# Starting the global queries' steps and the second unit of four heads four slots later in each chunk

## The chip, the cores and the metric

The kernel runs on one core of one Trainium2 chip. The metric is the device time of one execution in microseconds (us). A core has a tensor engine for matmuls (TensorE, PE in the profile), VectorE (DVE), ScalarE (ACT), GpSimd (POOL) and a sync engine (SP), which here issues nearly all DMAs. Each engine works through its own list of instructions in order, and waits for others by semaphores.

## The reference

Attention of 8 batches with 8 heads of 64, with 512 local and 32 global tokens each, and then a gated feed-forward layer over all 4608 tokens.

```python
k_all = concatenate([k_g, k_l]); v_all = concatenate([v_g, v_l])
out_g = matmul(sm(scale * matmul(q_g, k_all.T)), v_all)      # global queries see all keys
s_ll = where(abs(i - j) <= 32, scale * matmul(q_l, k_l.T), -1e9)
s_lg = scale * matmul(q_l, k_g.T)
out_l = matmul(sm(concatenate([s_lg, s_ll])), v_all)          # local queries: a band and the global keys
x = rows of concatenate([out_g, out_l])                       # 4608 x 512
xn = x / sqrt(mean(x * x) + 1e-6) * rms_g
g = xn @ w_gate                                               # 512 x 1536
out = (g / (1 + exp(-g)) * (xn @ w_val)) @ w_out
```

Here `sm` is a softmax with the row's maximum subtracted. `-1e9` stands for the mask outside the band.

## The kernel before

The 4608 rows go through the feed-forward layer in nine chunks: chunks 0 to 7 are the 512 local rows of each batch, chunk 8 the 256 global rows of all batches. While the matmuls of chunk c run, the attention for chunk c+1 is woven in between them. The order of every engine's instructions is the order in which the program writes them: chunk 0, with the attention of batches 0 and 1, by a list of names (`ORDER`), and the rest by the loop at the end of `attention_moe_kernel`, lines 1180 to 1209.

**Slots.** That loop has 72 slots for a chunk of 512 rows. Each slot writes one piece of the feed-forward layer, six matmuls of 128x512. Slots 0 to 47 are the twelve `f` (128 columns of the hidden layer each): two slots for the gate product, then ACT's `tanh` and DVE's `gate` (line 970); two for the value product, then DVE's `inner` (line 977), ACT's rounding to 16 bits (line 980) and POOL's rest (line 151). The products are on line 959. Slots 48 to 71 are four output blocks of six slots (line 1014), with a store after slots 53, 59, 65 and 71. After a slot's matmuls the attention steps that are due are written (`slot()`), and then the slot's own ACT and DVE work.

**Units and steps.** The attention of chunk c+1 is up to three units: local heads 0 to 3, the global queries of one batch, local heads 4 to 7. `UNIT` says from which slot a unit may start; after that each step follows its predecessors at fixed distances.

- A local unit: L and V (loads of q, k, v), S (scores, line 648, four slots after L), for each of four score banks M and N (masked minimum on DVE at line 599, exponentials on ACT at line 610), D (division, POOL, line 625) and T (transpose on DVE, line 630); A and B (the products with v in two parts, line 691, into four banks `a`); X and Y (DVE copies two of these banks each into a tile `x`, line 704, ACT squares it, line 708, and POOL adds up the squares, line 710).
- A global unit: GL (loads), GS (scores, line 762, into four banks `gs`), GM and GN (softmax, line 774 and 784), GT (transposes, line 805), GA (products with v, line 819), GD (division), GX (transpose into `xg`).

By these distances the steps of the three units stood so in each of chunks 1 to 6: first local unit L 2, S 6, A 19, B 21, X 22, Y 24; global unit GL 19, GS 23, GM 24, GN 26, GT 29, GA 33, GD 34, GX 36; second local unit L and V 33, S 37, T 43 to 49, A 50, B 52, X 53, Y 55. At the end of slot 55 what is left of the units is written at once. In chunk 7 two global units run alone, from slots 0 and 20 (`UNIT[2]`).

**Banks.** Scores, transposes and attention outputs share four PSUM banks (the pool tag `pa`). The global scores need all four, and so do a local unit's scores and its outputs.

**Norm.** The norm of chunk c+1 is written at slot 59 (DVE: transpose of the sum of squares and a reduce, lines 922 and 924), 61 (PE: sum over partitions, line 933, then DVE's root steps from line 934 on) and 66 (scaling, and splitting into two 16-bit halves `xh` and `xl`).

Of the kernel before, what the change touches and what calls it, by code (L numbers as in the profile page):

```python
# [65 lines left out]
def attention_moe_kernel(  # L66
# [24 lines left out]
    SPLIT, BGAP = 5, 2  # L91
    GG = (4, 5, 4, 3)
    NORM = (56, 59, 61, 66)
    UNIT = {2: (0, 20), 3: (2, 19, 33)}
    ST = 6
    con = ctx.enter_context(tc.tile_pool(name="con", bufs=1))
    pool = ctx.enter_context(tc.tile_pool(name="pool", bufs=2))
# [1012 lines left out]
    for c in range(NCH):  # L1110
# [3 lines left out]
        for i, un in enumerate(units):  # L1114
# [6 lines left out]
            for name, fn, pe, after in steps:  # L1121
                st = {"name": name, "fn": fn, "pe": pe, "c": c, "x": xi, "after": [], "at": None}
                st["from"] = UNIT[len(units)][i]
                for dep, gap in after:
# [211 lines left out]
```

## Time and profile before

| | |
|---|---|
| median of 3 runs | 981.94 us (979.61 to 983.16) |
| the profiled execution | 978.9 us, of which its span 977.1 us |
| granted TensorE clock, mean | 0.99 |
| TensorE products, line 959, xh and xl groups | 503.2 + 318.0 us |
| TensorE output blocks, line 1014 | 237.4 us |
| DMA | 88.24 MB, 90 GB/s over the span |

Busy times of matmuls overlap one another, because they are pipelined and their ends are modelled; distances between starts are the safer measure. A row of a timeline gives the start in us from the start of the span, the duration, the engine, the line, the operation, its output and inputs, the count, and in brackets the idle time ahead of it with what ended it. A row of the list of waits gives who waited for whom: us in total, times, the longest.

### The profile page before, as it was taken

How to read it: one execution, taken by the hardware profiler on the slowest of the kernel's cores; microseconds unless marked ns; L12 is line 12 of the kernel's file. 1: busy time of each engine (PE TensorE's matmuls, PEld its weight loads, DVE VectorE, ACT ScalarE, POOL GpSimd, SP SyncE). 2: the span in 40 equal slices, each digit the busy share in tenths (PEclk: the TensorE clock that was granted, in tenths of full speed). 3: DMA queues.
4: the chain of work that ended last, by engine and by line, in shares of the span. 5: the costliest groups of instructions: out<-in, count | busy, mean ns of one | idle time of the engine just before them, and what ended most of it. 6: DMA issues, size and time to landing. Idle time of an engine off the chain costs nothing.

```text
span 977.1 us, 22949 instructions
## 1 busy us (share of the span) xinstructions
PE 939.2 (96%) x9732; PEld 486.3 (50%) x9732; DVE 451.0 (46%) x1369; ACT 409.2 (42%) x1070; POOL 194.4 (20%) x183
## 2 busy tenths in 40 slices
PE   6588999999999999999999999999999999999998
PEld 4444455445544544445444544455444544444584
DVE  6999973444244344434345244434334344232331
ACT  7999982434124341435124441435034431332131
POOL 0000000232213231223113140323114140111120
PEclk9799999999999999999999999999999999999999
DMA  9962421800044000710053001700062002400100
GB/s 355 406 261 93 152 88 38 269 31 2 23 167 116 16 2 33 254 32 1 23 188 110 2 12 44 233 31 2 23 212 85 2 13 82 142 1 1 40 5 22
DMA packets 31254, 88.24 MB, mean 90 GB/s; under 512 B 3632, under 2 KB 3888, under 8 KB 31152
## 3 DMA queue, kind: packets, MB, share of 16 engines
q1 hardware_dynamic: 30720, 86.46, 25.7%
q8 instruction: 76, 1.25, 0.5%
q10 hardware_dynamic: 432, 0.33, 0.1%
q14 instruction: 26, 0.21, 0.1%
HBM read 77.86 MB, written 8.91 MB: 89 GB/s over the span
## 4 chain that ended last, share of the span: by engine, by line
PE 86%; DVE 6%; DMA 5%; ACT 2%; issue 1%; SPq 0%; ACTq 0%; DVEq 0%
PE p L959 48%; PE po L1014 24%; PE a L691 3%; PE po L1081 3%; PE s L648 2%; DMA k<-in_qk_dram 2%; DMA v<-in_vw_dram 1%; DMA wr<-in_w_in_dram 1%; PE ga L819 1%; PE gt L805 1%; PE gs L762 1%; DVE wf L366 1%; ACT wr L265 1%; DMA gkq<-in_gkq_dram 1%; DVE t L1050 1%
## 5 line engine op out<-in xcount | busy, mean ns | idle before, releaser
L959 PE MATMUL p<-xh,wf 128*128 128x512 f16 (+1 forms) x1728 | 503.2, 368 | 8.3 <-DVE t L1050 6.3
L959 PEld LDWEIGHTS <-wf 128*128 128x128 f16 x2592 | 250.5, 98 | 280.1 <-issue 20.4
L959 PE MATMUL p<-xl,wf 128*128 128x512 f16 (+1 forms) x864 | 318.0, 368 | 0.0
L1014 PE MATMUL po<-wo,h 128*128 128x512 f16 x1080 | 237.4, 379 | 0.0
L151 POOL TENSOR_TENSOR h<-t,h 128x512 f16<-128x512 f32 (+1 forms) x96 | 105.2, 1095 | 565.9 <-ACT h L980 528.6
L1014 PEld LDWEIGHTS <-h 128*128 128x128 f16 x1080 | 104.8, 98 | 123.7
L970 DVE SCALAR_TENSOR_TENSOR t<-t,p 128x512 f32<-128x512 f32 (+1 forms) x96 | 62.8, 654 | 223.3 <-ACT t L969 223.3
L980 ACT CAST h<-t 128x512 f16<-128x512 f32 (+1 forms) x96 | 56.5, 588 | 164.8 <-DVE t L977 164.8
L969 ACT ACTIVATE t<-p,half_inv 128x512 f32<-128x512 f32 (+1 forms) x96 | 62.9, 656 | 115.8 <-PE p L959 100.5
L977 DVE SCALAR_TENSOR_TENSOR t<-t,c_h,p 128x512 f32<-128x512 f32 (+1 forms) x96 | 68.1, 710 | 78.6 <-PE p L959 78.6
L610 ACT ACTIVATE e<-e,sm 128x128 f32<-128x128 f32 x192 | 74.8, 390 | 40.6 <-DVE sm L599 40.6
L625 POOL TENSOR_TENSOR e<-e,sm 128x512 f32<-128x512 f32 x48 | 49.9, 1039 | 45.5 <-DVE sm L624 32.8
L1025 ACT ACTIVATE o<-po,kk 128x512 f32<-128x512 f32 x15 | 10.3, 688 | 114.2 <-PE po L1014 114.2
L599 DVE CUSTOM_DVE_ANT_0 e<-s,maskb 128x128 f32<-128x128 f32 x192 | 45.0, 281 | 5.6 <-PE s L648 5.6
L1027 DVE TENSOR_SCALAR o<-po,kk 128x512 f32<-128x512 f32 x15 | 11.3, 751 | 64.5 <-PE po L1014 64.5
L708 ACT ACTIVATE sq<-x 128x512 f32<-128x512 f32 x24 | 15.1, 628 | 55.7 <-DVE x L704 55.5
L630 DVE STREAM_TRANSPOSE et<-e 128x512 f32<-128x512 f32 x48 | 34.0, 708 | 7.5 <-POOL e L625 7.5
L691 PEld LDWEIGHTS a<-et,v 32*64 32x64 f32 x2112 | 31.0, 130 | 11.0 <-issue 10.2
L610 ACT ACTIVATION_READ_ACCUMULATOR e<-e,sm 128x1 f32 x192 | 35.8, 186 | 0.0
L691 PE MATMUL a<-et,v 32*64 32x96 f32 (+3 forms) x2112 | 35.5, 258 | 0.0
L704 DVE COPY x<-a 128x256 f32<-128x256 f32 x48 | 17.5, 416 | 38.2 <-PE a L691 38.2
L1081 PE MATMUL po<-wo,h 128*128 128x512 f16 x144 | 32.4, 379 | 0.0
(320 smaller groups left out, 743.5 us busy)
## 6 DMA issues: line engine op xcount, KB each, us to landing
wr<-in_w_in_dram SPq DMA_DIRECT2D x24, 512.0 KB, 10.0
k<-in_qkb_dram SPq DMA_DIRECT2D x24, 448.0 KB, 7.5
gkq<-in_gkq_dram SPq DMA_DIRECT2D x16, 576.0 KB, 8.0
out_dram<-o SPq DMA_DIRECT2D x34, 256.0 KB, 2.0
v<-in_vb_dram SPq DMA_DIRECT2D x24, 352.0 KB, 5.1
v<-in_vw_dram SPq DMA_DIRECT2D x16, 512.0 KB, 9.6
gv<-in_gv_dram SPq DMA_DIRECT2D x16, 448.0 KB, 10.9
wr<-in_w_out_dram SPq DMA_DIRECT2D x12, 512.0 KB, 4.1
```

The lines of the kernel that those rows point to most:

```text
L151: nc.gpsimd.tensor_tensor(dst, a, b, ALU.subtract)
L599: nc.vector.tensor_tensor_reduce(out=e[:, g, :], in0=ps[:, g * P : (g + 1) * P], in1=late["mask"][:, m * P : (m + 1) * P], scale=-0.125, s ...
L610: nc.scalar.activation(e[:, g, :], e[:, g, :], AF.Exp, bias=sm[:, 0, j + g : j + g + 1], scale=-1.0, accum_out=sm[:, 1, j + g : j + g + 1],)
L625: nc.gpsimd.tensor_tensor(e, e, r.unsqueeze(2).to_broadcast([P, 4, P]), ALU.mult)
L691: nc.tensor.matmul(o, st["v"][x][r, m * D : (m + 1) * D], e, start=(m == blocks[0]), stop=(m == blocks[-1]), skip_group_check=True,)
L959: nc.tensor.matmul(ps[:, :n], wf[f][:, a, o : o + P], ch[z][k][:, :n], start=(k == 0 and i == 0), stop=(k == NK - 1 and i == 2),)
L969: nc.scalar.activation(t[:, :n], pg[:, :n], AF.Tanh, scale=half_inv[:, f : f + 1])
L970: nc.vector.scalar_tensor_tensor(t[:, :n], t[:, :n], 1.0, pg[:, :n], ALU.add, ALU.mult)
L977: nc.vector.scalar_tensor_tensor(t[:, :n], t[:, :n], c_h[:, f : f + 1], pv[:, :n], ALU.mult, ALU.mult)
L980: nc.scalar.copy(h[:, 0, :n], t[:, :n])
L1014: nc.tensor.matmul(ps[0], ch["h", f][:, a, j * P : (j + 1) * P], wo[f][:, z, :], start=(f == 0 and q == 0), stop=(f == NF - 1 and q == 2),)
L1081: nc.tensor.matmul(po[j], ch["h", f][:, a, j * P : (j + 1) * P], wo[f][:, z, :], start=(f == 0 and q == 0), stop=(f == NF - 1 and q == 2),)
```

## The change

One line: in chunks 1 to 6 the global unit may start from slot 23 instead of 19, and the second local unit from slot 37 instead of 33.

```diff
-    UNIT = {2: (0, 20), 3: (2, 19, 33)}
+    UNIT = {2: (0, 20), 3: (2, 23, 37)}
```

By the fixed distances GS stands at slot 27, GX at 40, the second unit's S at 41, T at 47 to 53, A at 54. B would be due at 56, X at 57 and Y at 59; all three are written at the end of slot 55. Work, tiles and buffers stay as they are.

The first place is on DVE in chunk 1, from the copies of the first unit's step X to the first softmax step of the global unit (`a` are the local outputs in PSUM, `gs` the global scores, `p_5` and `p_6` the products of f=5 and f=6). Before:

```order
L704 COPY x_0_2602<-a_2474 128x256
L977 SCALAR_TENSOR_TENSOR t_2592<-t_2592,c_h,p_5_2595 128x512
L704 COPY x_1_2645<-a_2475 128x256
L704 COPY x_1_2645<-a_2476 128x256
L774 ISA ge_2614,gsm_2613<-gs_2615,zeros 128x272
L774 ISA gsm_2613 128x1
L774 ISA ge_2614,gsm_2613<-gs_2616,zeros,gsm_2613 128x272
```

and now:

```order
L704 COPY x_0_2592<-a_2474 128x256
L977 SCALAR_TENSOR_TENSOR t_2582<-t_2582,c_h,p_5_2585 128x512
L704 COPY x_1_2623<-a_2475 128x256
L704 COPY x_1_2623<-a_2476 128x256
L970 SCALAR_TENSOR_TENSOR t_2635<-t_2635,p_6_2616 128x512
L977 SCALAR_TENSOR_TENSOR t_2635<-t_2635,c_h,p_6_2638 128x512
L774 ISA ge_2652,gsm_2651<-gs_2653,zeros 128x272
```

The copies stay behind the `inner` of f=5; the readers of the global scores moved behind the whole of f=6.

On PE the same place, with the semaphores that the rows wait for: the last product of the slot ahead of the global scores, and the first score of each half. Before:

```order
L959 MATMUL p_5_2595<-xh_2172,wf_957 128x512
L762 MATMUL gs_2615<-gkq_2517 32x272 [waits DMAHW3_49,DVE_49]
L762 MATMUL gs_2617<-gkq_2517 32x272 [waits DVE_49]
...
L762 MATMUL gs_2616<-gkq_2517 32x272 [waits DVE_49,PE_49]
L762 MATMUL gs_2618<-gkq_2517 32x272 [waits DVE_49,PE_49]
```

and now:

```order
L959 MATMUL p_6_2638<-xh_2172,wf_1124 128x512
L762 MATMUL gs_2653<-gkq_2603 32x272 [waits DMAHW3_49,PE_49]
L762 MATMUL gs_2655<-gkq_2603 32x272 [waits PE_49]
...
L762 MATMUL gs_2654<-gkq_2603 32x272 [waits DVE_49,PE_49]
L762 MATMUL gs_2656<-gkq_2603 32x272 [waits DVE_49,PE_49]
```

The scores follow the products of f=6 instead of those of f=5, and their first half no longer has a wait for DVE.

The last place is on ACT in chunk 1, from the second unit's last step before its outputs to the norm's split (`po` are output blocks 0 and 2, `x_2` and `x_3` the second unit's outputs). Before:

```order
L980 CAST h_2992<-t_3022 128x512
L708 ACTIVATE sq_3177<-x_2_3174 128x512
L1025 ACTIVATE o_3180<-po_3044,kk 128x512
L708 ACTIVATE sq_3199<-x_3_3196 128x512
L1025 ACTIVATE o_3286<-po_3233,kk 128x512
```

and now:

```order
L619 ACTIVATE sm_2870<-sm_2870 128x4
L1025 ACTIVATE o_3082<-po_3028,kk 128x512
L708 ACTIVATE sq_3193<-x_2_3190 128x512
L708 ACTIVATE sq_3199<-x_3_3196 128x512
L1025 ACTIVATE o_3286<-po_3233,kk 128x512
```

The store of block 0 is written ahead of both squares, which now come together, and the last of the softmax (line 619) comes after the last `f` instead of before it. On SP the order of the DMAs is the same before and now.

## The prediction

> **What bounds the kernel now.** First the page: the share of each engine, then the list of who waited for whom on the tensor engine alone, then one chunk in windows.
>
> ```profile
> PE 939.2 (96%) x9732; PEld 486.3 (50%) x9732; DVE 451.0 (46%) x1369; ACT 409.2 (42%) x1070; POOL 194.4 (20%) x183
> PEclk9799999999999999999999999999999999999999
> PE gs L762 <- DVE x L704: 3.9, 6, 0.7
> PE p L959 <- issue: 1.4, 1, 1.4
> 281.90:390.60 108.70, 108.05 (x1167) 53.51 (x1166) 45.23 (x145) 38.84 (x115) 28.10 (x25) 1.00 0.22 72
> ```
>
> TensorE (PE) is busy 96% of the span at its full granted clock; the digits below 9 stand at the start. From 174 us to the end its list has only the two rows shown (us in total, times, longest). The last row is one of the six chunks that the change touches, from window start to end: length, PE busy, weight loads, DVE, ACT, POOL, granted clock, DMA share and GB/s. PE is idle in it for 0.65 us out of 108.70. So VectorE (DVE), ScalarE (ACT) and GpSimd (POOL), at 45, 39 and 28 us, bound nothing by their work; the change can gain only where PE stalls, six times at the global queries' scores (line 762), and can lose only where it makes PE stall anew.
>
> Here is that stall in the same chunk: PE's timeline, then DVE's, then PE's at the second global unit of the last-but-one chunk, which no local unit runs beside.
>
> ```profile
> 316.98 0.38 PE L959 MATMUL p<-xh,wf 128*128 128x512 f16 x1
> 317.29 0.69 PE L762 MATMUL gs<-gkq 64*32 64x272 f32 x16
> 318.62 1.02 PE L762 MATMUL gs<-gkq 64*32 64x272 f32 x16 [0.65 <-DVE x L704]
> 319.57 0.39 PE L959 MATMUL p<-xh,wf 128*128 128x512 f16 x1
> ...
> 317.39 0.75 DVE L977 SCALAR_TENSOR_TENSOR t<-t,c_h,p 128x512 f32<-128x512 f32 x1 [1.80 <-PE p L959]
> 318.06 0.75 DVE L704 COPY x<-a 128x256 f32<-128x256 f32 x2
> ...
> 861.35 1.15 PE L762 MATMUL gs<-gkq 64*32 64x272 f32 x32
> 862.43 0.39 PE L959 MATMUL p<-xh,wf 128*128 128x512 f16 x1
> ```
>
> The scores come as 32 records. After the first 16 PE stops until DVE has copied the last two local output banks out of PSUM (step Y, issued in slot 24). Those copies stand behind the `inner` multiplication of line 977, which needs the products of slot 23 itself, and the scores were queued right after those products. So PE waits for work that it releases only just before.
>
> **The change part by part.** A slot is six 128x512 matmuls, and I take its price from this unit's end:
>
> ```profile
> 355.32 4.05 PE L1014 MATMUL po<-wo,h 128*128 128x512 f16 x18
> 359.30 1.54 PE L691 MATMUL a<-et,v 32*64 32x256 f32 x80
> 360.77 2.76 PE L1014 MATMUL po<-wo,h 128*128 128x512 f16 x12
> 363.47 1.31 PE L691 MATMUL a<-et,v 32*64 32x96 f32 x96
> 364.71 11.83 PE L1014 MATMUL po<-wo,h 128*128 128x512 f16 x54
> 376.37 0.29 PE L933 MATMUL ss<-nt,same 128*128 128x16 f32 x2
> ```
>
> The 54 matmuls take 376.37 - 364.71 = 11.66 us from start to start: 0.216 us each, 1.30 us a slot.
>
> *Global scores, slot 23 to 27.* No matmul is added or taken away. The copies of step Y stay at slot 24; at 318.06 to 318.81 they will be done 3 slots (3.9 us) before the scores come up. The wait goes. Its price is not the 0.65 us of the wait row but what the group takes from its first matmul to the next product: 319.57 - 317.29 = 2.28 us with the wait, 862.43 - 861.35 = 1.08 us without. In both places the product ahead starts 0.31 us before the group, so the comparison is fair. The stall costs 1.20 us, and in six chunks 7.2 us. What could be late next: the scores' own input, and PE's waits behind them. Line 970 of f=6 and all later products sit 4 slots apart from the global steps as before, since one f takes four slots; a shift by four meets the same phase of the gates. Products of f=6 now carry waits on DVE of their own (the wait of the scores covered them), for `inner` of f=5, which ends at 318.14, two slots before the second product group that needs the bank: hidden.
>
> *Why 1.20 and not 0.65.* [...] This trace speaks for starts: two groups of the same 32 records differ by 1.20.
>
> *Loads.* The steps GL, L and V are moved four slots as well, with five, four and two DMA issues. Their order on the sync engine's (SP's) queue stays as it is, and that queue doesn't run by slots:
>
> ```profile
> 284.96 0.90 SPq L741 DMA_DIRECT2D gkq<-in_gkq_dram  x2
> 285.90 1.84 SPq L747 DMA_DIRECT2D gv<-in_gv_dram  x3
> 293.24 0.43 SPq L580 DMA_DIRECT2D k<-in_qkb_dram  x1
> 314.72 1.61 SPq L588 DMA_DIRECT2D v<-in_vb_dram  x2
> gkq<-in_gkq_dram SPq DMA_DIRECT2D x16, 576.0 KB, 8.0
> gv<-in_gv_dram SPq DMA_DIRECT2D x16, 448.0 KB, 10.9
> ```
>
> The global tiles are requested at 285, 32 us before their scores, and land in 8 to 11 us. The second local unit's last load is issued at 314.72, when the first unit's step B, which doesn't move, frees its tile. Cost nothing; if the queue did follow the slots, the scores would still have their gap of four slots, 5.2 us, against 8.0, and 2.8 us x 6 would be lost. Nothing in SP's queue holds it back, so I don't count that.
>
> *Second local unit, scores slot 37 to 41, A 50 to 54, B 52 to 55, X 53 to 55, Y stays at 55.* Up to A everything moves by four slots, 5.2 us. From slot 48 on PE does output blocks and DVE and ACT have no gates, so the softmax ends no later against A than before:
>
> ```profile
> 357.61 0.71 DVE L630 STREAM_TRANSPOSE et<-e 128x512 f32<-128x512 f32 x1 [0.61 <-POOL e L625]
> 364.68 1.42 DVE L704 COPY x<-a 128x256 f32<-128x256 f32 x4 [6.37 <-PE a L691]
> 366.27 0.69 ACT L1025 ACTIVATE o<-po,kk 128x512 f32<-128x512 f32 x1 [0.17 <-PE po L1014]
> 366.86 0.62 ACT L708 ACTIVATE sq<-x 128x512 f32<-128x512 f32 x1
> 366.25 2.63 POOL L710 TENSOR_TENSOR sq<-sq,sq 128x512 f32<-128x512 f32 x2 [7.36 <-PE po L1014]
> 368.91 0.71 DVE L922 STREAM_TRANSPOSE st<-sq 128x512 f32<-128x512 f32 x1 [2.81 <-POOL sq L710]
> 369.66 0.69 DVE L924 TENSOR_REDUCE nt<-st 128x16 f32<-128x512 f32 x1
> ```
>
> The last transpose ended at 358.32, 1.0 us ahead of A; that distance can only grow. Worth: 0.
>
> B loses its distance: PE's blocks after it shrink from 9 slots to 6 before the norm's sum (line 933, slot 61). On this chunk's clock, without the gain: 42 matmuls from 355.32 are 9.07 us, A from 364.4 takes 360.77 - 359.2 = 1.56, a slot 1.30, B 1.35, so B ends at 368.6 and the sum stands at 376.4, 7.8 us on. What must fit in is the chain copies, squares, POOL adds, transpose, reduce: in the rows above from 364.71 to 370.35, 5.64 us. Slack falls from 6.0 to 2.1 us; still cover, so 0. ACT's store `o` of block 0 now comes ahead of both squares instead of between them, which takes nothing from the chain. DVE's store of block 1 follows the reduce at about 374.3, and the sum's reader (line 934) comes at 376.7. If the cover went, each us beyond it would cost 6 us. For an upper end I take the first unit's slower chain: its copies start at 314.84 and its add ends at 321.26, 6.4 us, with other work between; with 1.5 for transpose and reduce it makes 7.9, 0.1 beyond: 0.6 us in all.
>
> ```profile
> 314.84 0.75 DVE L704 COPY x<-a 128x256 f32<-128x256 f32 x2
> 319.99 1.27 POOL L710 TENSOR_TENSOR sq<-sq,sq 128x512 f32<-128x512 f32 x1
> ```
>
> **The sum.** Range of the removed stall 3.9 to 7.2 us, of the closer norm 0 to -0.6, all else 0; I take 7.2, because it compares whole groups. The profiled execution lasted 978.9 us (span 977.1, 1.8 around it) and becomes 971.7. The median of the runs is 981.94, 3.0 above it (the three go from 979.61 to 983.16); less 7.2 that is **974.7 us**, 0.73% faster.
>
> **The rivals.**
> - *Only the idle row is real*: 3.9 us, 978.0. For it: the second 16 records may always take that long when the array restarts elsewhere. Against: 1.08 for the whole group at 861. Chance 0.12.
> - *The wait moves on*: PE meets as much elsewhere, at the second unit's scores or at the gates, because the same 45 us of DVE work are now packed into slots 27 to 55. 981.9. Against: the pattern is shifted by exactly one f, and its tail goes to slots without gates. For: DVE's last wait in the unit, at 357.61, is only 0.61 us, so it is not far from being the late one. Chance 0.06. The change does nothing else than it says: all six units move, so a rival of that kind has no place.
> - *The norm becomes late* (slower): place line 933, slot 61. It decides from a chain of 7.8 us. Were it 9.9 us, PE would stand 2.1 us in each chunk, 12.6 against 7.2 gained: 987.3. For it: slack falls to a third. Against: nothing in the chain grows, and the slowest like it is 7.9. Chance 0.04.
>
> **How the numbers follow.** The forecast has 0.78. A measurement of this kernel can tell about 0.5%, so faster means under 977.0. Runs scatter by about 1.8 us, so the forecast's own range is 972.3 to 977.1, with some 0.93 of it under the bound; with a little of the first rival, faster is 0.74. Within 0.5% hold the rest of the forecast, most of the first rival and all of the second, 0.22; slower 0.04. The range reaches to the first rival and its scatter, 972.0 to 978.9.
>
> **What would show it.** The row of line 762 waiting for line 704 is gone from PE's list, and each of the six score groups takes about 1.1 us to the next product. The chunk's pitch falls by 1.2 us. The sum of line 933 starts right behind its block's matmuls, with DVE's reduce done about 2 us before. If a PE wait for DVE on line 933, 691 or 959 appears, the second or third rival holds; if groups still take 1.6 us or more, the first. A score group that waits for gkq would refute the reading of the queue.

## The result and the profile after

| | before | after |
|---|---|---|
| median of the runs | 981.8 us (979.61 to 983.16, 4 runs) | 975.04 us (972.81 to 976.36, 4 runs) |
| ratio | | 0.9931 (95% interval 0.9904 to 0.9957) |
| the profiled execution, its span | 978.9, 977.1 us | 976.36, 974.6 us |
| global scores, first matmul to next product, six chunks | 2.28 to 2.29 us | 1.08 us |
| distance of the norm's sums of two neighbouring chunks | 108.73 us | 107.54 us |

The forecast was 974.7 us. First the list of TensorE's (PE's) waits after 150 us in the profile after, then PE's timeline at the global scores of chunk 2 and at two of the norm's sums, and one chunk in a window (length, then busy time of PE, weight loads, DVE, ACT, POOL, granted clock, DMA share, GB/s).

```profile
PE p L959 <- issue: 3.3, 1, 3.3
PE a L691 <- issue: 0.6, 1, 0.6
PE s L648 <- DMA k<-in_qkb_dram: 0.4, 1, 0.4
...
326.19 1.15 PE L762 MATMUL gs<-gkq 64*32 64x272 f32 x32
327.27 0.39 PE L959 MATMUL p<-xh,wf 128*128 128x512 f16 x1
...
594.13 0.29 PE L933 MATMUL ss<-nt,same 128*128 128x16 f32 x2
701.67 0.29 PE L933 MATMUL ss<-nt,same 128*128 128x16 f32 x2
...
393.00:500.60 107.60, 107.60 (x1167) 53.53 (x1166) 45.42 (x146) 39.06 (x115) 28.11 (x25) 1.00 0.22 73
```

The wait of line 762 for line 704 is gone. The 32 records come as one group and the next product starts 327.27 - 326.19 = 1.08 us after its first, the price that the undisturbed group had. The two sums stand 107.54 us apart. In the profile before they stood so:

```profile
593.84 0.29 PE L933 MATMUL ss<-nt,same 128*128 128x16 f32 x2
702.57 0.29 PE L933 MATMUL ss<-nt,same 128*128 128x16 f32 x2
```

that is 108.73 us. This chunk lost 1.19 us, six at that rate lose 7.1 us, and PE is busy in all of the 107.60 us of its window.

The end of the second unit, in the same chunk as in the prediction, on PE and then on DVE:

```profile
357.84 9.23 PE L1014 MATMUL po<-wo,h 128*128 128x512 f16 x42
367.00 1.54 PE L691 MATMUL a<-et,v 32*64 32x256 f32 x80
368.47 1.47 PE L1014 MATMUL po<-wo,h 128*128 128x512 f16 x6
369.87 1.48 PE L691 MATMUL a<-et,v 32*64 32x96 f32 x96
371.29 7.95 PE L1014 MATMUL po<-wo,h 128*128 128x512 f16 x36
379.07 0.29 PE L933 MATMUL ss<-nt,same 128*128 128x16 f32 x2
...
364.56 0.71 DVE L630 STREAM_TRANSPOSE et<-e 128x512 f32<-128x512 f32 x1 [1.22 <-POOL e L625]
371.34 1.42 DVE L704 COPY x<-a 128x256 f32<-128x256 f32 x4 [6.08 <-PE a L691]
376.29 0.69 DVE L924 TENSOR_REDUCE nt<-st 128x16 f32<-128x512 f32 x1
```

The last transpose ends at 365.27, 1.7 us ahead of A (before: 1.0). The reduce ends at 376.98, 2.1 us ahead of the sum, and the sum follows its block without a gap.

The profiled execution lost only 2.5 us of its span, not 7.2, for reasons that lie elsewhere. At slot 6 of chunk 1, ahead of everything that moved, PE stands after the first unit's scores, with no releaser in the profile ("issue"):

```profile
179.69 2.06 PE L648 MATMUL s<-k,q 64*32 64x128 f32 x128
185.06 0.39 PE L959 MATMUL p<-xh,wf 128*128 128x512 f16 x1 [3.31 <-issue]
...
185.00:188.00 3.00, 2.94 (x9) 1.14 (x10) 0.71 (x2) 0.00 (x0) 0.00 (x0) 0.61 1.02 223
```

From 179.69 to the next product it takes 5.37 us here and 3.45 in the profile before, 1.9 more, and the clock granted from 185 to 188 us is 0.61; the first eleven matmuls behind the stall take another 1.7 us more than in the profile before. With 1.0 us more at step B of chunks 1 and 2 (below) and 0.8 at the first scores of chunk 2, where a load of k landed late, this comes to 5.4 us. Chunk 7 was 0.4 us shorter than before, nearly all of it at its first global scores (1.38 us instead of 1.81), which leaves 5.0 against the 4.7 us that are missing. Whether the stall belongs to the change is asked of the experiments.

### The profile page after: what moved, and what is told of

It reads as the page before. It is cut to its first block, busy times and chain, and to the rows that moved or that the text cites. A ratio compares the mean times of both kernels' runs of the same rounds, so it can differ in the third digit from the quotient of the medians.

```text
span 974.6 us, 22959 instructions
## 1 busy us (share of the span) xinstructions
PE 937.4 (96%) x9732; PEld 486.5 (50%) x9732; DVE 452.2 (46%) x1369; ACT 410.7 (42%) x1070; POOL 194.5 (20%) x183
## 3 DMA queue, kind: packets, MB, share of 16 engines
q8 instruction: 76, 1.25, 0.5%
## 4 chain that ended last, share of the span: by engine, by line
PE 86%; DVE 6%; ACT 5%; DMA 2%; issue 1%; ACTq 0%; SPq 0%; DVEq 0%
PE p L959 48%; PE po L1014 24%; PE a L691 4%; PE po L1081 3%; PE s L648 2%; ACT wr L265 1%; PE ga L819 1%; PE gs L762 1%; PE gt L805 1%; DMA wr<-in_w_in_dram 1%; DVE wf L366 1%; DMA k<-in_qkb_dram 1%; PE a L523 1%; DMA ident<-in_eye_dram 1%; DVE t L1050 1%
## 5 line engine op out<-in xcount | busy, mean ns | idle before, releaser
L710 POOL TENSOR_TENSOR sq<-sq,sq 128x512 f32<-128x512 f32 x18 | 22.8, 1266 | 49.5 <-ACT sq L708 49.0
```

## The experiments

The "pitch" is the distance of the norm's sums (line 933) of chunks 4 and 5, in the steady part. All times are medians; the ratio is to the runs of the kernel before on the same chip.

| run | median us | ratio, 95% interval | score group us | pitch us |
|---|---|---|---|---|
| step Y one slot earlier, units unmoved | 974.39 | 0.9933 (0.9915 to 0.9951) | 1.08 | 107.52 |
| second local unit alone later | 981.69 | 1.0004 (0.9992 to 1.0016) | 2.28 | 108.72 |
| the changed kernel again | 974.8 | 0.9946 (0.9929 to 0.9963) | 1.08 | 107.52 |
| the changed kernel, A one slot later | 972.98 | 0.9921 (0.9906 to 0.9936) | 1.08 | 107.01 |
| the kernel before again | 981.89 (one run) | | 2.28 | 108.74 |
| norm's sum three slots earlier | 988.53 | 1.0067 (1.0052 to 1.0083) | 1.08 | 109.47 |
| both units twelve slots later | 1006.71 | 1.0247 (1.0226 to 1.0267) | 1.08 | 112.73 |
| A later, and A and B in one group | 974.99 | 0.9936 (0.9919 to 0.9953) | 1.08 | 106.81 |
| both units one slot later | 975.13 | 0.9943 (0.9922 to 0.9964) | 1.08 | 107.89 |
| global unit alone later | 978.94 | 0.9972 (0.9957 to 0.9988) | 1.08 | 108.30 |

### The wait taken away without moving a unit

```diff
-            ("Y", lambda: take(1), 0, [("X", 2)]),
+            ("Y", lambda: take(1), 0, [("X", 1)]),
```

> Step Y of every local unit comes one slot after X instead of two; UNIT stays as before. In the first unit its two copies then stand on DVE ahead of the inner of f=5, so the global scores at slot 23 find their banks free without being moved. Theory (the copies' wait is the whole gain, 1.20 us per group): group of line 762 takes 1.08 us to the next product instead of 2.28, wait row gone, 7.2 us saved, 974.6 us, as in the changed kernel, though no unit starts later. Rival 1 (the gain comes from the second unit's softmax standing in slots without gates): nothing saved, 981.8 us. Rival 2 (only the 0.65 us of the idle row is real): 977.9 us.

DVE's timeline of this run, and PE's, at the global scores of chunk 2:

```profile
314.74 1.41 DVE L704 COPY x<-a 128x256 f32<-128x256 f32 x4
317.29 0.75 DVE L977 SCALAR_TENSOR_TENSOR t<-t,c_h,p 128x512 f32<-128x512 f32 x1 [1.14 <-PE p L959]
...
317.18 1.15 PE L762 MATMUL gs<-gkq 64*32 64x272 f32 x32
318.26 0.39 PE L959 MATMUL p<-xh,wf 128*128 128x512 f16 x1
```

All four copies now stand ahead of line 977 and end at 316.15, before the scores. The group takes 1.08 us at slot 23, and 7.2 us are saved (981.62 to 974.39) with every unit in its old place. So the order of two copies and one `inner` on DVE was the whole cause, and the slots without gates bring nothing that the pitch would show: it is 107.52 us here and in the second profile of the changed kernel.

### The second unit alone

```diff
-    UNIT = {2: (0, 20), 3: (2, 19, 33)}
+    UNIT = {2: (0, 20), 3: (2, 19, 37)}
```

> UNIT[3] = (2, 19, 37): only the second unit of local heads moves, the global unit stays. Theory: the global scores still wait, 2.28 us per group, nothing saved, 981.8 us within 0.2%; the norm's sum still meets 2.1 us of cover. Rival 1 (gate-free slots for the second unit): 975 us with the stall still there. Rival 3 (the later end of the second unit costs something that the changed kernel paid out of its gain): slower than before, by 0.6 us or more.

The time is that of before within 0.1%, and the stall stands where it stood, here PE in chunk 2:

```profile
320.38 0.69 PE L762 MATMUL gs<-gkq 64*32 64x272 f32 x16
321.71 1.02 PE L762 MATMUL gs<-gkq 64*32 64x272 f32 x16 [0.65 <-DVE x L704]
322.66 0.39 PE L959 MATMUL p<-xh,wf 128*128 128x512 f16 x1
```

In the medians the later end of the second unit neither gains nor costs anything, as the prediction's zero for that part says. The profile shows a small cost all the same: step B of the second unit takes 1.80 and 1.42 us in chunks 1 and 2, and 1.24 in every other chunk, 0.7 us in all. In the run with step Y earlier it takes 1.24 in all six.

### The global unit alone

```diff
-    UNIT = {2: (0, 20), 3: (2, 19, 33)}
+    UNIT = {2: (0, 20), 3: (2, 23, 33)}
```

> UNIT[3] = (2, 23, 33): only the global unit moves. GS loses its wait (1.08 us, 7.2 us saved), but the global unit's last steps now overlap the second unit's start: GA 37, its scores S 38 (all four banks), GX 40 (one bank). Theory: PE meets a new wait for DVE at line 648 or 840, of 0.3 to 2 us in each of six chunks, so part of the gain is given back: 976 to 985 us. Rival (the banks are free in time anyway, the second unit need not move): 974.6 us with no such wait.

The scores lose their wait, and 0.8 us a chunk comes back (pitch 108.30 against 107.52). The size was as expected, the place only in part: the transpose GX waits 0.22 us, and the rest is at the second unit's A, which is now one slot later in the pattern of four (scores at slot 38 instead of 37):

```profile
582.22 2.07 PE L691 MATMUL a<-et,v 32*64 32x256 f32 x80
584.22 2.12 PE L1014 MATMUL po<-wo,h 128*128 128x512 f16 x9
...
582.00 0.71 DVE L630 STREAM_TRANSPOSE et<-e 128x512 f32<-128x512 f32 x1 [2.10 <-POOL e L625]
```

A takes 2.00 us there to the next product, against 1.47 in the changed kernel. No row of the list of waits shows it, but DVE's last transpose ends at 582.71, after A has begun. So the second unit has to move with the global one, not for its own gain.

### Both units one slot later

```diff
-    UNIT = {2: (0, 20), 3: (2, 19, 33)}
+    UNIT = {2: (0, 20), 3: (2, 20, 34)}
```

> UNIT[3] = (2, 20, 34): both units one slot later instead of four. GS stands at slot 24, one slot (1.3 us) behind the products of slot 23. The copies of step Y end 1.5 us behind those products, and only the second half of the scores needs their banks, 0.5 us into the group. Theory: no wait is left, group 1.08 us, 7.2 us saved, 974.6 us; the other three slots of the change do nothing. Rival (it takes the move by a whole f, since another phase meets the gates): a new PE wait for DVE and over 976 us.

One slot is enough for the scores (1.08 us). But the expectation that nothing else happens was wrong: A of the second unit takes 1.83 to 1.85 us instead of 1.47, and the pitch is 0.37 above that of the changed kernel, 2.2 us in six chunks. The medians (975.13 and 974.8) are too close to tell that; the profiles do. The last transpose shows why:

```profile
575.47 1.91 PE L691 MATMUL a<-et,v 32*64 32x256 f32 x80
577.30 2.76 PE L1014 MATMUL po<-wo,h 128*128 128x512 f16 x12
...
575.08 0.71 DVE L630 STREAM_TRANSPOSE et<-e 128x512 f32<-128x512 f32 x1 [2.09 <-POOL e L625]
```

It ends at 575.79, after A has begun. Two of the 80 matmuls of A start ahead of that and 78 behind it, so the group waits within itself. The move by four slots, one whole `f`, keeps the phase and so has no such cost.

### The changed kernel and the kernel before once more

> The changed kernel once more: 975.0 us, six groups of line 762 at 1.08 us, chunk pitch 107.5 us. At the start of chunk 1, before anything moved, its first profile has a PE stall put down to issue of 3.3 us and half clock behind it, where before has 1.4 us. If that is scatter from execution to execution, this profile shows another length (between 0 and 4 us) and the span follows it; if it belongs to the changed program, it shows 3.3 us and half clock again.

> The kernel before, profiled once more. The four profiles with the second unit four or more slots later have a PE stall put down to issue of 3.3 to 3.6 us at slot 6 of chunk 1; before had 1.4 and the run with step Y early 2.0. If the stall scatters by itself, this profile of the same program as before shows another length than 1.4 us, up to 4; if the later units lengthen it, 1.4 to 2.0 us again.

The changed kernel gives 974.8 us. As for the stall at slot 6 of chunk 1: here are the rows behind it in the second profile of the kernel before, and then in that of the changed kernel, each with a window behind the stall.

```profile
185.13 0.39 PE L959 MATMUL p<-xh,wf 128*128 128x512 f16 x1 [2.98 <-issue]
185.00:188.00 3.00, 2.87 (x9) 1.12 (x10) 0.94 (x4) 0.16 (x1) 0.00 (x0) 0.67 1.05 252
...
186.25 0.39 PE L959 MATMUL p<-xh,wf 128*128 128x512 f16 x1 [3.40 <-issue]
186.00:189.00 3.00, 2.75 (x13) 1.28 (x14) 1.25 (x6) 0.46 (x1) 0.00 (x0) 1.00 1.03 238
```

The same program of before shows 1.39 us in one execution and 2.98 with a lower clock in another, and its span grows with it from 977.1 to 980.1. So the stall scatters by itself and is no part of the change; in the twelve profiles it goes from 1.39 to 3.64 us. What it goes with is in the last section.

### A one slot later behind the last transpose

```diff
-            ("A", lambda: values(blocks[:SPLIT]), 1, [("T3", 1), ("V", 4)]),
+            ("A", lambda: values(blocks[:SPLIT]), 1, [("T3", 2), ("V", 4)]),
```

> The changed kernel, and step A of local units one slot later behind the last transpose (first unit: A 20, B 22, X 23, Y 25; second unit: A and B both at the end of slot 55). Theory (PE waits briefly for the last transpose at the first unit's A, which takes 1.78 us there and 1.56 in the second unit): the first A falls to 1.56 us, 1.3 us saved in six chunks, 973.7 us. Rival (1.78 us belongs to that place among products): 975.0 us. Rival (A and B at slot 55 back to back make X or the norm late): over 975.5 us, and a PE wait for DVE at line 933.

This is the best version measured, 972.98 us. It uses what the comparison of groups showed beside the change: A of the first unit takes 1.69 us to the next product and that of the second 1.47. One slot later the first falls to 1.47 too, and A and B of the second unit, now next to each other, take 2.51 instead of 1.47 + 1.24. Together 0.4 to 0.5 us a chunk, as the pitch of 107.01 shows. Six chunks at 0.51 would be 3.1 us; the medians show 1.8. In chunks 1 and 2 the second unit's group takes 3.92 and 3.01 us instead of 2.51, with stalls that have no releaser, so the expectation missed a cost here.

### A and B in one group

```diff
-            ("A", lambda: values(blocks[:SPLIT]), 1, [("T3", 2), ("V", 4)]),
-            ("B", lambda: values(blocks[SPLIT:]), 1, [("A", BGAP)]),
+            ("A", lambda: values(blocks), 1, [("T3", 2), ("V", 4)]),
+            ("B", lambda: None, 0, [("A", 0)]),
```

> The changed kernel with A one slot later behind the last transpose, as in the run with A later (973.0 us), and B's products written in one group with A's in both units: no other products between them. Theory (each group of small matmuls costs about 0.2 us to start and end, as 2.51 us for A and B together against 1.47 + 1.24 show): one group less in the first unit, 0.2 us a chunk, 971.8 us. Rival (the longer block makes a gate or a product late): a PE wait for DVE at line 959, 974 us or more.

In the steady part the theory holds: the pitch falls by another 0.20 us, to 106.81, and in three other chunks to 106.70. The time rises all the same, to 974.99 us, and neither theory had it: in chunks 1 and 2 each of the four groups stalls for 1.0 to 1.4 us, with no releaser ("issue"), and takes 3.7 to 4.1 us instead of 2.51. Here is the list's row for all four, and the first of them:

```profile
PE a L691 <- issue: 5.2, 4, 1.4
202.88 2.49 PE L691 MATMUL a<-et,v 32*64 32x256 f32 x171
206.73 0.31 PE L691 MATMUL a<-et,v 32*64 32x32 f32 x5 [1.36 <-issue]
```

In the changed kernel, where one slot is left between A and B of the second unit, the same stall is small: B takes 2.05 and 1.42 us in chunks 1 and 2 in one profile and 1.50 and 1.24 in the other, against 1.24. In both profiles of the kernel before, with two slots between, it takes 1.24 or 1.25. That is a cost of the change that the prediction didn't have, 0.3 to 1.0 us in all.

### The norm's sum earlier

```diff
-    NORM = (56, 59, 61, 66)
+    NORM = (56, 57, 58, 66)
```

> The changed kernel with the norm's DVE part at slot 57 and its sum on PE at slot 58 instead of 59 and 61: the cover of the chain from B to the reduce falls from 36 matmuls (7.8 us) to 18 (3.9 us). Theory (chain of 5.6 us, cover decides): PE waits for DVE at line 933, 1.75 us a chunk and with the restart up to 2.3, in six chunks 10.5 to 14 us: 985 to 989 us (the global chunk's norm may add up to 3). Rival (the reduce is early anyway, the slack is larger than 2.1 us): under 978 us, no wait at line 933.

988.53 us, 13.7 above the changed kernel. PE and DVE at the sum of chunk 2:

```profile
371.99 4.06 PE L1014 MATMUL po<-wo,h 128*128 128x512 f16 x18
377.83 0.37 PE L933 MATMUL ss<-nt,same 128*128 128x16 f32 x2 [1.78 <-DVE nt L924]
377.00 0.69 DVE L924 TENSOR_REDUCE nt<-st 128x16 f32<-128x512 f32 x1
```

From 371.99, the end of B, to the end of the reduce it is 5.70 us (expected 5.6), and 18 matmuls cover 3.9. PE waits 1.41 to 1.94 us in each of the six chunks, and the pitch grows by 1.95. So the cover was real, and so is the wait that the third rival names; in the changed kernel it lies 2.1 us away.

### Twelve slots later

```diff
-    UNIT = {2: (0, 20), 3: (2, 23, 37)}
+    UNIT = {2: (0, 20), 3: (2, 31, 45)}
```

> UNIT[3] = (2, 31, 45), twelve slots later than before: the second unit's scores stand at slot 49, and its steps from M3 on and A, B, X, Y are all written at the end of slot 55. Theory (the softmax of a unit takes about 10 us from its scores to the last transpose, bound by ACT; the room is six slots, 7.8 us): PE waits at A, about 2 us in each of six chunks, 987 us (980 to 995); the global scores stay at 1.08 us. Rival (the tail without gates has room enough): 975 us.

1006.71 us. The place was right, the price 2.6 times as large as expected: 5.2 us a chunk instead of 2.

```profile
594.74 3.40 PE L1014 MATMUL po<-wo,h 128*128 128x512 f16 x15
600.35 0.61 PE L691 MATMUL a<-et,v 32*64 32x256 f32 x2 [2.21 <-issue]
602.29 3.29 PE L691 MATMUL a<-et,v 32*64 32x256 f32 x174 [1.33 <-DVE et L630]
605.51 6.83 PE L1014 MATMUL po<-wo,h 128*128 128x512 f16 x28
...
599.54 0.71 DVE L630 STREAM_TRANSPOSE et<-e 128x512 f32<-128x512 f32 x1 [0.82 <-POOL e L625]
601.52 0.71 DVE L630 STREAM_TRANSPOSE et<-e 128x512 f32<-128x512 f32 x1 [1.22 <-POOL e L625]
...
604.00:607.00 3.00, 3.00 (x99) 1.99 (x87) 1.42 (x4) 0.80 (x2) 0.06 (x1) 0.54 0.02 5
```

PE stands 2.21 us ahead of A, then 1.33 for a transpose: 3.5 us, not 2. The first wait is put down to issue, but it ends 0.10 us after the last transpose but one (600.25), as the second ends 0.06 us after the last (602.23), so both are waits for the softmax. From the start of the scores at 588.21 to there it is 14.0 us, not the 10 of the expectation. And the clock granted behind that, in the window from 604 to 607 us, is 0.54, and the rest of the group runs slower (174 of its 176 matmuls take 602.29 to 605.51, 3.22 us, where all 176 took 2.51 in the run with A one slot later); that cost was in no expectation. Six slots between a unit's scores and its A, 7.8 us, are too few for its softmax of 14.0 us. The move by four slots leaves this distance as it was, at 13 slots.

## Why the prediction was right

- **The stall and its place**: right. With the copies ahead of line 977 the wait goes at an unchanged slot; with the second unit alone moved it stays.
- **1.20 us instead of the idle row's 0.65**: right. The groups fell from 2.28 to 1.08 us, and the chunk by 1.19. The first rival (3.9 us, 978.0) falls. The idle row saw 0.65 of 1.20 us, and the partial waits within A (1.69 and 1.84 against 1.47 us) appear in no row at all. That starts give the price is borne out by the chunk: it went from 108.73 us to 107.52 in the second profile of the changed kernel, 1.21 us, as the groups did by starts (2.29 to 1.08).
- **Loads at no cost**: right so far as the trace goes; no score group waited for gkq in chunks 1 to 6. One load of k came 0.43 us late in chunk 2 in one of the two profiles of the changed kernel, and 0.34 in the run twelve slots later. It belongs to the first unit, which didn't move. In the two profiles of the kernel before it landed 1.0 and 0.5 us ahead of the same scores, so there was little to spare; why it was late stays open.
- **A keeps its distance**: right, 1.7 us against 1.0. The reason, a move by one whole `f`, was shown by the moves that break it, in which the last transpose ends after A has begun: one slot costs 0.37 us a chunk at A, the global unit alone 0.53.
- **B's shrinking cover**: right to 0.1 us. The slack is 2.1 us, the chain 5.7 against 5.64, and taking the cover away made PE wait at line 933.
- **The sum**: 7.2 us forecast; 6.8 by the medians, 7.1 by the steady chunks. Missing from the sum was the stall of 0.3 to 1.0 us at step B in chunks 1 and 2; it is too small to show in the medians. The profiled execution came out at 976.4 instead of 971.7, mostly because the stall at the start of chunk 1 was 1.39 us in the profile of before, the shortest of the twelve, and 3.31 us with a lower clock behind it in the profile after. The forecast of the median didn't rest on that execution alone, which is why it held.

## What to carry to other kernels

A wait is priced by the distance from the group's first start to the next group's, against the same group elsewhere without the wait; the idle row showed about half of it here (0.65 of 1.20 us), and a wait inside a group of small matmuls not at all (A took 1.84 us instead of 1.47). Where an engine waits for copies out of a shared bank, look first at what stands ahead of the copies on their own engine: putting them ahead of one instruction did as much here as moving two units (974.39 and 974.8 us). In a woven schedule with a period, move work by whole periods (one slot instead of four cost 0.37 us a chunk here), and check the cover of the last chain before the end. Where PE stalls without a releaser, look in the trace for a packet of the queue that the page names "instruction", landing just before the stall ends: here 20 of 26 such stalls ended 1.2 to 1.6 us after one.

## What the runs showed of the hardware

- The same program stalls for 1.4 us in one execution and 3.0 in another at one place of PE, with no releaser, while the DMA share (the times of the packets that start in the window, as a share of 16 engines) is 1.04 (181 to 184 us in the first profile of before, 182 to 184 in the second). The traces show what these stalls go with. The page of every profile has a DMA queue that it names "instruction", here that of before (packets, MB, share):

```profile
q8 instruction: 76, 1.25, 0.5%
```

  PE has 19464 matmuls and weight loads, 256 for each of these packets of 16 KB. At slot 6 of chunk 1 such a packet landed at 181.63 us in the first profile of before and at 183.62 in the second, and PE went on 1.51 us later in both; in the profile after one landed at 183.45, and PE went on 1.61 us later. In the twelve profiles there are 26 stalls of PE at lines 959 and 691 without a releaser, after 150 us and longer than 0.25 us. Six are the waits for a transpose in the run twelve slots later; each of the other 20 ends 1.2 to 1.6 us after a packet of this queue has landed. In the run with A and B in one group the records from stall to stall are 1.99, 4.97, 3.98 and 4.97 times 256, and the packets that landed ahead of the stalls stand 2, 5, 4 and 5 apart in their queue. No run changed these packets, so it was not shown whether PE waited for them.
- Of the eight profiles in which that stall was 2.98 us or more, five show a lower clock right behind it (0.61 and 0.67 over the windows above) and three full clock, one of them after 3.40 us (1.00 in the other window above). The lower clock is 0.50 from 185.65 to 189.06 us in the profile after, 3.41 us long, and the windows of the other four give 3.4 us as well. In the profiles before and after all changes of the granted clock lie whole multiples of 3.41 us apart; in the latter it is lower from 96.90 us and again from 185.65, 26 times 3.41 us on. The length of a wait alone didn't tell whether a lower clock followed: 3.40 us had none behind it, 2.98 had one. In the run with the norm's sum earlier a PE wait of 1.94 us had one behind it (0.66 over 4 us), while behind five of 1.41 to 1.78 us the clock was 1.00. In the run twelve slots later, where PE waits 2.21 and 1.33 us at A in each of six chunks, it was 0.50 to 0.62 over 3 us behind all of them. What decides was not shown. The wait, and a window that begins right behind it:

```profile
815.94 0.39 PE L933 MATMUL ss<-nt,same 128*128 128x16 f32 x2 [1.94 <-DVE nt L924]
816.00:820.00 4.00, 4.00 (x14) 1.68 (x15) 3.22 (x14) 0.00 (x0) 0.00 (x0) 0.66 0.02 4
```

- Groups of small matmuls that stand closer together than in the kernel before stall without a releaser in chunks 1 and 2, but not in later chunks, at the same places of the same code order: by 1.36, 1.31, 1.05 and 1.43 us in the run with A and B in one group, by 0.56 at step B of chunk 1 in the profile after. The larger of these stalls are among the 20 above: A and B together are 352 of PE's records in 2.5 us, where a slot has 12 in 1.3 us. Why later chunks are free of the stall was not shown.
